# Where a finished sum is copied, when raw weights are loaded, and what stands in front of transpositions: three edits to a grouped-attention and Mish kernel

## The chip, the cores and the metric

The kernel runs on one core of a Trainium2 chip. A core has five engines that each take their instructions in the order of their own queue: TensorE (PE in the profile; PEld is its weight load), VectorE (DVE), ScalarE (ACT), GpSimd (POOL) and SyncE (SP), which here issues the DMAs. They tell each other by semaphores. Matrix products are written to PSUM, eight banks of 128 partitions x 512 floats; everything else lies in SBUF. The metric is the time of one execution in microseconds (us); a run's figure is compared with runs of the kernel before on the same chip.

## The reference, cut to what matters

```python
xn = layernorm(A_x)                              # 2048 x 512
q = xn @ wq; k = xn @ wk; v = xn @ wv            # 32 heads of 16; one k and v for all heads
p = softmax(q k^T / 4)                           # 32 x 2048 x 2048
s = (p v, heads side by side) @ wo               # 2048 x 512
h = xn @ w1 + b1                                 # 2048 x 1792
g = silu((h * tanh(softplus(h))) @ w2)           # Mish between the layers
out = A_x + s * g
```

All is float32. A dense product is kept precise by splitting both operands into a high and a low part and adding three partial products (`TERMS`), so a group of four 128-row weight blocks is 12 matrix products.

## The kernel before, in words

**Attention.** Queries are cut in 4 chunks of 512 rows (`C`) and 8 groups of 4 heads, so there are 32 passes ("heads" below, index v). A pass has 16 steps; in a step PE makes four score products `e` (line 966), four products `m` (L994) whose row maxima DVE takes (L998) for a pass that comes later, and the value products `pv` (L1050) of two steps before. ACT takes the exponential of each score (L971) into one of 14 tiles `pts`. The value products of a pass accumulate over its 16 steps in one PSUM bank. That pool, `ps_v`, has one buffer: the next pass's first value products can only start when the sum of the pass before has been read out. `o_out` does this: a copy on ACT (L1059, `os<-pv`), eight small DMAs out of `os` on SP (L1068), and, three steps later, jobs for ACT and POOL that divide by the row sums.

**Dense work.** The projections, both layers of the Mish branch and the output projection run as groups of 12 or 15 products (`xps`, L113 for a whole product, L117 for half of one). They are laid between the attention's products: a half of 64 rows runs beside a score or maximum product, which also uses 64 rows. A group of 12 takes four single steps, 6 halves in each; a group of 15 takes a "unit", four steps written out as two halves (`UNIT`). A group's `post` reads its sum out by ACT or DVE. Groups start at steps divisible by four and come from two queues, query groups first.

**The order.** The whole order is made by a Python planner when the program is built. Each engine has a list; steps, due times (`at`, `later`) and estimated times of POOL (`busy`) and SP (`sp_t`) say when something is emitted. The engines then run their lists in order.

**Weights.** Weights are loaded raw (`rawwq`, `rawws`, `rawwb`: two buffers together, `RAWS = 2`, at most one for each kind), split into a high part and a low part (in the lead-in by ACT and POOL, later by POOL alone, L165 and L170) and, in the main loop, stored split in DRAM, so that later chunks load them split. Split tiles sit in rings: 1 for `wq`, 2 for `ws` (first Mish layer), 5 for `wb` (second layer and output). Before the change `load` does nothing while the ring's next tile is still used by a group (`its[n - RING[tag]].users`), so the raw load of a first-layer block waits for the split tile of two blocks before. `pump` splits what has arrived and issues loads, once per step.

**The lead-in.** Up to about 91 us the planner works with `Task`s: statistics, scaling, transpositions of the input (`x_transpose`, 4 to a block, into the banks of `e`), key and value projection, value transpositions (`v_transpose`). PE takes, in this order of preference, a task, a pair of `m` products, or, where its next task is over 0.35 us away, three dense products ("X") or a warming product without use (`warm`, L1283). The main loop begins when 44 `m` products per side are through and the first pass's rows have been moved.

**Ends of passes.** In a single step, the last line of the step's branch calls `o_out` right after the pass's last value products. In a unit the first half does, after its last value products. The tail (the last 22 steps) has its own calls.

Of the kernel before, what the change touches and what calls it, by code (L numbers as in the profile page):

```python
# [36 lines left out]
X_US = 13.0  # L37
# [30 lines left out]
class Task:  # L68


    def __init__(self, eng, us, fn, deps=(), lat=0.1, at=0.0, prio=0):
        self.eng, self.us, self.fn, self.deps, self.lat, self.at, self.prio = eng, us, fn, list(deps), lat, at, prio
        self.end = None

# [49 lines left out]
def block_kernel(ctx: ExitStack, tc: tile.TileContext, x, wq, wk, wv, wo, w1, b1, w2, out):  # L124
# [13 lines left out]
    lead = {}  # L138
# [7 lines left out]
    def step_of(us):  # L146
        return base[0] + (us - base[1]) / STEP_US
# [248 lines left out]

    def arrived(tag):
        k, n = todo[tag]
        return k < n and items[tag][k].step + 1 <= (step[0] if lead else max(step[0], step_of(busy[0])) + 0.3)

    def home(tag, k):
# [22 lines left out]
    kept = {}  # L424
# [18 lines left out]
    def load(tag):  # L443
        its = items[tag]
        k, n = todo[tag]
        if tag == "wx" and m1_done.get((NC - 2, NFT - 1)) is None or lead and tag == "wq" and n > 1:
            return
        if n == len(its) or n >= RING[tag] and its[n - RING[tag]].users or lead and tag == "wb" and n and now[0] < kept_at.get(3, 1e9):
            return
        it = its[n]  # L450
        if n == k and kept.get(it.key):
            it.tile = home(tag, n)
            sp.dma_start(f(it.tile), kept[it.key])
            it.ready = math.ceil(2 * (sp_at(0.5) + 1.6)) / 2
            todo[tag][:] = n + 1, n + 1
        elif n - k < NRAW[tag] and raws[0] < RAWS:
            r = sb.tile([P, D], F32, tag="raw", name=f"raw{tag}{n}", bufs=RAWS)
            if len(it.src.shape) == 3:
                sp.dma_start(r.rearrange("p (t n) -> p t n", t=NDT), it.src)
            else:  # L460
                sp.dma_start(r, it.src)
            it.raw, it.step = r, (lead["arrive"]() if lead else sp_at(0.45))
            raws[0] += 1
            todo[tag][1] += 1

    def pump():
        for tag in items:
            while arrived(tag):
                split(tag)
            load(tag)  # L470

    held = [None]
    halves = [0]
# [127 lines left out]
    def unit(s, h):  # L601


        g, t = cur["g"], s + 2 * h
        xs = deque(g.mms)
        v, r = divmod(s, 16)
        es = deque((1 - h, r + j // 2, j % 2) for j in range(8))
        late = []
        relay = None

        def x_one():
            i = xs.popleft().half(cur["ps"], h)
            if len(xs) == len(g.mms) - 1 and h:
                tc.add_manual_dep(i.ins, cur["relay"].ins.name, mybir.DependencyInfo(
                    mybir.DependencyClass.Sync, mybir.DependencyReason.DATA), reason="other half of the bank")
            if h and g.dve and len(xs) == HOLD:
                held[0] = []
            if not xs and h:
                cur["n"] = len(g.mms)
                finish()  # L620
                for top in held[0] or ():
                    top()
                held[0] = None

        due(t)
        for n, op in enumerate(UNIT):
            if n == 8:
                due(t + 0.5)
                pump()
                due(t + 1)  # L630
            if op == "0":
                m_one(h)
                op = "E"
            elif xs:
                x_one()
            if op == "E":
                e = es.popleft()
                if len(es) > 1:
                    score(v, *e)()
                else:  # L640
                    late.append(score(v, *e))
            elif op in "Mm":
                relay = m_one(1 - h, op == "m")
        assert not xs and not es
        cur["relay"] = relay
        act_jobs(2 + (len(jobs) > 2))
        due(t + 1.5)
        for n in range(2):
            pv(t + n - 2)
            if n == 0:  # L650
                for fn in late:
                    fn()
        if t % 16 == 0:
            o_out((t - 16) // 16)

    qt_of = {}
    xt_done = {}
# [563 lines left out]
    for c0, c1 in ((0, 1), (1, 2), (2, 4)):  # L1221
        z = slice(4 * c0, 4 * c1)
        na = task("DVE", 0.2, lambda z=z: norm_a(z), st[z], prio=c0 and 1)
        nb = task("ACT", 0.45, lambda z=z: norm_b(z), [na])
        nrm = task("DVE", 0.8, lambda z=z: norm_c(z), [nb], prio=2 * c0 and 1)
        for c in range(c0, c1):
            xs, his = [], []
            for t in range(4 * c, 4 * c + 4):
                sc = task(*(("ACT", 0.72), ("DVE", 0.4))[c == 0], lambda t=t: x_scale(t), [nrm])
                tr = task("PE", 0.6, lambda t=t: x_transpose(t), [sc])  # L1230
                if c == 0:
                    hi = task("ACT", 0.55, lambda t=t: x_high(t), [tr])
                    lo = task("DVE", 0.65, lambda t=t: x_low(t), [hi])
                    bank("e", 3, tr, [lo])
                    xs.append(lo)
                else:
                    lo = task("ACT", 0.62, lambda t=t: x_copy(t), [tr])
                    bank("e", 3, tr, [lo])
                    xs.append(lo)
            los = xs  # L1240
            if c:
                his = [task("ACT", 0.98, lambda c=c, k=k: x_high2(c, k), xs, prio=2) for k in range(2)]
                los = [task("POOL", 2.5, lambda c=c, k=k: x_low2(c, k), [his[k]]) for k in range(2)]

            def xt_ok(c=c):
                xt_done[c] = step[0]
            if c < 2:
                task("POOL", 0.0, xt_ok, los)
            else:
                kept_0 = task("SP", 0.5, lambda c=c: xt_keep(c, 0), his)  # L1250

                def keep_low(c=c):
                    xt_keep(c, 1)
                    landed(2 * KEEP_US)
                    kept_at[c] = max(now[0] + 2, dma_t[0]) + 1
                task("SP", 0.5, keep_low, los + [kept_0])
            if c == 0:
                qp = task("PE", 2.8, lambda: fill(12), xs)
                xs = [qp]
            kus = 0.9 if c else 0.7  # L1260
            k0 = kp = task("PE", kus, lambda c=c: k_proj(c, (0,)), xs)
            for dt in range(1, 4):
                kp = task("PE", kus, lambda c=c, dt=dt: k_proj(c, (dt,)), [kp], lat=0.0)
            kv_done = kp
            kh = task("ACT", 0.59, lambda c=c: k_high(c), [kp])
            kl = task("DVE", 0.68, lambda c=c: k_low(c), [kh])

            def mv(c=c):
                k_move(c)
                kready[c] = now[0] + 2.6  # L1270
            moved = task("SP", 0.5, mv, [kl])
            if c == 0:
                lead["moved"] = moved
            vc = task("ACT", 0.59, lambda c=c: v_copy(c), [kp])
            bank("v", 1, k0, [kl, vc])
            vtr = task("PE", 0.5, lambda c=c: v_transpose(c), [vc])
            vo = task("DVE", 0.22, lambda c=c: v_out(c), [vtr])
            bank("v", 1, vtr, [vo])

# [25 lines left out]
    while True:  # L1305
# [58 lines left out]
        elif k == "J":  # L1364
            tag = next((g for g in ("wq", "ws", "wb") if arrived(g) and busy[0] + E0 < s + (4.5 if g == "ws" else 0.5)), None)
            n = ran[0]
            if tag:
                split(tag)
                T["ACT"] = s + 0.6
            else:  # L1370
                gap[0] = 0
                if not plan["POOL"]:
                    act_jobs(1)
                T["ACT"] = s + (0.65 if ran[0] > n else 0.15)
        else:
            plan[e].remove(k)
            k.fn()
            T[e] = max(s, T[e]) + k.us + (0.15 if e == "PE" and kind[0] == "M" else 0)
            k.end = T[e]
            if e == "PE":  # L1380
                kind[0] = "T"
# [30 lines left out]
    for s in range(NS + 2000):  # L1412
# [12 lines left out]
        if inm or cur["chunk"]:  # L1425
# [3 lines left out]

            def em(k):  # L1430
                n = m_sides(1 - h, k // 2) if inm else 0
                x = deque(lambda i=i: e_one(s, i) for i in range(4))
                y = deque(lambda: m_one(1 - h) for _ in range(n))
                r = [[], []]
                for op in EM:
# [12 lines left out]
            if s >= 2:  # L1448
                pv(s - 2)
                if (s - 1) % 16 == 0 and s > 1:  # L1450
                    o_out((s - 17) // 16)
        elif PAIRS[0] <= s < PAIRS[1]:
            due(s)
            if s % 2 == 0:
# [47 lines left out]
```

## Time and profile before

| | |
|---|---|
| median of 3 runs | 1587.54 us (1586.33 to 1588.32) |
| profiled execution | 1587.25 us, span 1585.5 us |
| granted TensorE clock | 0.996 of full speed |
| busy share of the span | PE 99%, PEld 55%, DVE 85%, ACT 82%, POOL 39% |
| chain that ended last | PE 93%, ACT 2%, DVE 2% |
| DMA | 126.76 MB, mean 80 GB/s |

In a row of the timeline stand: start in us from the span's start, length in us, engine, line, operation, tiles written and read, shapes, count, and in brackets the idle time before it and what ended that. A row of the windows has the window, its length, and for PE, PEld, DVE, ACT and POOL the busy us with the count of instructions, then the granted clock, the DMA share and GB/s. In the chain a row is start, length, engine, tile and line. A source row has the shortest, median and longest duration in ns, then the first and last start.

### The profile page before, as it was taken

Reading aid. Unit: us, or ns where it says so; the run is one execution under the profiler, and the core shown is the slowest. Engines: PE = TensorE matmul, PEld = TensorE weight load, DVE = VectorE, ACT = ScalarE, POOL = GpSimd, SP = SyncE. Lnnn points to the kernel's source line nnn. Section 1 sums busy time; section 2 is a strip of 40 time slices with the busy share of each in tenths; the row PEclk is TensorE's granted clock in tenths of the full one; section 3 lists DMA queues with packets and bytes.
Section 4 is the critical chain, followed back from the end, with each engine's and each line's share of the span. In section 5 each row is a group of like instructions: output and inputs, shape, how many; then the busy total and the mean of one; then the engine's idle time right before and its main releaser. Section 6 shows DMA issues by size and latency. Waiting matters only on the chain.

```text
span 1585.5 us, 31218 instructions
## 1 busy us (share of the span) xinstructions
PE 1567.0 (99%) x11649; PEld 876.2 (55%) x11649; DVE 1342.0 (85%) x2299; ACT 1296.2 (82%) x2492; POOL 622.6 (39%) x630
## 2 busy tenths in 40 slices
PE   8999999999999999999999999999999999999998
PEld 5455655665555565565555556556655555655643
DVE  8988887888988988888899988888889999888821
ACT  5469878878989787887988888798798888879786
POOL 3787527617446221450542323054044232405212
PEclk9999999999999999999999999999999999999999
DMA  5432114224132133311302231142221313121110
GB/s 163 147 105 85 58 47 131 84 58 144 41 122 70 55 104 97 112 41 49 109 23 97 85 100 34 49 161 95 71 84 32 105 53 107 29 71 58 32 63 27
DMA packets 73158, 126.76 MB, mean 80 GB/s; under 512 B 21488, under 2 KB 34800, under 8 KB 72496
## 3 DMA queue, kind: packets, MB, share of 16 engines
q1 hardware_dynamic: 73008, 124.78, 25.2%
q8 instruction: 92, 1.51, 0.4%
q14 instruction: 58, 0.48, 0.1%
HBM read 75.83 MB, written 27.26 MB: 65 GB/s over the span
## 4 chain that ended last, share of the span: by engine, by line
PE 93%; ACT 2%; DVE 2%; POOL 1%; DMA 1%; issue 0%; SPq 0%; DVEq 0%; POOLq 0%; ACTq 0%
PE xps L117 42%; PE pv L1050 31%; PE m L994 12%; PE e L966 6%; PE xps L113 2%; ACT pts L971 1%; DVE mb L998 1%; PE kp L309 1%; PE wop L113 1%; ACT pts L212 0%; PE warm L1283 0%; DMA pts<-in_dram 0%; DVE st L234 0%; DMA rawws<-in_dram 0%; PE xp L270 0%
## 5 line engine op out<-in xcount | busy, mean ns | idle before, releaser
L998 DVE TENSOR_REDUCE mb<-m 128x1 f32<-128x512 f32 x2048 | 1266.0, 681 | 171.5 <-PE m L994 112.1
L971 ACT ACTIVATE pts<-e 128x512 f32<-128x512 f32 x2042 | 1062.2, 606 | 217.7 <-PE e L966 152.4
L994 PE MATMUL m<-ks,qt 48*128 48x512 f32 (+1 forms) x2048 | 842.8, 427 | 0.6 <-DVE mb L998 0.3
L966 PE MATMUL e<-qt,ks 64*128 64x512 f32 x2048 | 746.4, 408 | 4.3 <-ACT pts L971 3.6
L1050 PE MATMUL pv<-pts,vaug 128*32 128x512 f32 x4084 | 530.8, 603 | 0.0
L994 PEld LDWEIGHTS m<-ks,qt 48*128 48x128 f32 (+1 forms) x2048 | 368.0, 185 | 115.6 <-DVE mb L998 67.3
L966 PEld LDWEIGHTS e<-qt,ks 64*128 64x128 f32 x2048 | 371.9, 186 | 28.9 <-ACT pts L971 16.9
L117 PE MATMUL xps<-xt,ws 64*128 64x512 f32 x1230 | 341.4, 410 | 0.2 <-POOL ws L170 0.2
L117 PEld LDWEIGHTS xps<-xt,ws 64*128 64x128 f32 x1230 | 212.0, 185 | 202.5 <-ACT pts L971 133.3
L117 PE MATMUL xps<-wbs,act 64*128 64x512 f32 x1248 | 313.5, 396 | 0.0
L117 PEld LDWEIGHTS xps<-wbs,act 64*128 64x128 f32 x1248 | 226.8, 185 | 63.5 <-ACT pts L971 29.3
L1050 PEld LDWEIGHTS pv<-pts,vaug 128*32 128x32 f32 x4084 | 88.1, 108 | 151.7 <-issue 143.7
L180 POOL TENSOR_SCALAR t<-t 128x512 f32<-128x512 f32 x56 | 34.4, 614 | 298.0 <-ACT t L732 298.0
L170 POOL TENSOR_TENSOR hb<-hb,t 128x512 f32<-128x512 f32 x56 | 72.2, 1289 | 120.5 <-ACT t L745 68.4
L117 PE MATMUL xps<-xt,wq 64*128 64x512 f32 x336 | 94.3, 414 | 0.0
L117 PEld LDWEIGHTS xps<-xt,wq 64*128 64x128 f32 x336 | 58.7, 187 | 55.5 <-ACT pts L971 36.9
L117 PE MATMUL xps<-wbs,ot_all 64*128 64x512 f32 x288 | 79.3, 408 | 0.0
L117 PEld LDWEIGHTS xps<-wbs,ot_all 64*128 64x128 f32 x288 | 49.5, 184 | 46.9 <-ACT pts L971 28.5
L170 POOL TENSOR_TENSOR act<-hb,act 128x512 fp32r<-128x512 f32 x56 | 72.2, 1289 | 4.7
L170 POOL TENSOR_TENSOR hb<-hb,u 128x512 f32<-128x512 f32 x56 | 72.3, 1290 | 4.4
L170 POOL TENSOR_TENSOR u<-u,t 128x512 f32<-128x512 f32 x56 | 71.8, 1283 | 4.7
L170 POOL TENSOR_TENSOR oc<-oc,sc 128x512 f32<-128x512 f32 (+1 forms) x16 | 20.6, 1288 | 103.0 <-ACT sc L1078 63.0
(122 smaller groups left out, 821.0 us busy)
## 6 DMA issues: line engine op xcount, KB each, us to landing
ws<-w SPq DMA_DIRECT2D x36, 512.0 KB
wbs<-w SPq DMA_DIRECT2D x35, 512.0 KB
qt<-qh SPq DMA_DIRECT2D x256, 32.0 KB
w<-wbs SPq DMA_DIRECT2D x14, 512.0 KB
wq<-wq SPq DMA_DIRECT2D x14, 512.0 KB
w<-ws SPq DMA_DIRECT2D x14, 512.0 KB
wbs<-wo SPq DMA_DIRECT2D x12, 512.0 KB
rawwb<-in_dram SPq DMA_DIRECT2D x21, 256.0 KB
```

The source lines that it names most:

```text
L113: self.pe.matmul(ps, self.lhs(), self.rhs(), start=(self.k == 0), stop=(self.k == self.tot - 1))
L117: i = self.pe.matmul(ps, self.lhs()[o], self.rhs()[o], start=(self.k == 0 and self.halves == 0), stop=(self.k == self.tot - 1 and self.hal ...
L170: eng.tensor_tensor(out=o, in0=a, in1=b, op=op)
L180: pool.tensor_scalar(o, o, lim, 0.0, op0=ALU.min, op1=ALU.max)
L309: pe.matmul(kp_of[c], wkf[:, dt], xf_of[c][dt // 2][:, dt % 2], start=(dt == 0), stop=(dt == 3))
L966: pe.matmul(e, ks[o:o + 64, P * k:P * (k + 1)], q[o:o + 64, p], start=True, stop=True)
L971: x = act.activation(dst, e, AF.Exp, scale=0.25)
L994: pe.matmul(m, q[o, p, P * t:P * (t + 1)], ks[o, C * kb:C * (kb + 1)], start=True, stop=True)
L998: return dve.reduce_max(out=mb_of[v][:, kb, z:z + 1], in_=m, axis=AX.X)
L1050: pe.matmul(o[32 * j:32 * j + 32], vaug[:, k], pt, start=(k == 0), stop=(k == 15))
```

## The change: what it does

It has three parts.

1. A `Task` gets a mark `fill`. It is set for the input transpositions of chunks 1 to 3 and the value transpositions of chunks 1 to 3. When the planner emits such a task on PE and a dense group is running, or one may begin, it emits one dense product in front of it and charges 0.25 us.
2. `load` goes on for first-layer weights (`ws`) that must be loaded raw, though the split tile is still used; `arrived` now says no while it is used, so the split alone waits.
3. `o_out` is no longer called where a pass ends, but put into a queue. In single steps the next step takes it from there before its third score; in units the next half takes it after all its scores, maxima and dense halves, ahead of ACT's jobs and the half's value products. The tail's own calls stay.

```diff
-    def __init__(self, eng, us, fn, deps=(), lat=0.1, at=0.0, prio=0):
+    def __init__(self, eng, us, fn, deps=(), lat=0.1, at=0.0, prio=0, fill=False):
+        self.fill = fill
...
     def arrived(tag):
         k, n = todo[tag]
+        if k >= RING[tag] and items[tag][k - RING[tag]].users:
+            return False
...
-        if n == len(its) or n >= RING[tag] and its[n - RING[tag]].users or lead and tag == "wb" and n and now[0] < kept_at.get(3, 1e9):
+        if n == len(its) or lead and tag == "wb" and n and now[0] < kept_at.get(3, 1e9):
             return
         it = its[n]
+        taken = n >= RING[tag] and its[n - RING[tag]].users
+        if taken and (tag != "ws" or kept.get(it.key)):
+            return
...
+    outs = deque()
+
+    def put_out(fn):
+        outs.append(fn)
+
+    def take_out():
+        if outs:
+            outs.popleft()()
...
         assert not xs and not es
         cur["relay"] = relay
+        take_out()
         act_jobs(2 + (len(jobs) > 2))
...
         if t % 16 == 0:
-            o_out((t - 16) // 16)
+            put_out(lambda: o_out((t - 16) // 16))
...
-                tr = task("PE", 0.6, lambda t=t: x_transpose(t), [sc])
+                tr = task("PE", 0.6, lambda t=t: x_transpose(t), [sc], fill=c > 0)
...
-            vtr = task("PE", 0.5, lambda c=c: v_transpose(c), [vc])
+            vtr = task("PE", 0.5, lambda c=c: v_transpose(c), [vc], fill=c > 0)
...
             plan[e].remove(k)
+            if k.fill and (cur["g"] is not None or not waiting and begun[0] < 1 + (s - 18) / X_US):
+                fresh = cur["g"] is None
+                if not fresh or begin():
+                    begun[0] += fresh
+                    fill(1)
+                    T[e] = max(T[e], s - 0.2) + 0.25
             k.fn()
...
-                x = deque(lambda i=i: e_one(s, i) for i in range(4))
+                x = deque(lambda i=i: (i == 2 and take_out(), e_one(s, i))[1] for i in range(4))
...
                 if (s - 1) % 16 == 0 and s > 1:
-                    o_out((s - 17) // 16)
+                    put_out(lambda s=s: o_out((s - 17) // 16))
```

## The prediction

> **What bounds the kernel now.** I read the page first (span, busy shares, chain), then the PE and ACT timelines around one handover of the value sum, then the stretches where a step is longer than its neighbours, then the lead-in by windows.
>
> ```profile
> span 1585.5 us, 31218 instructions
> PE 1567.0 (99%) x11649; PEld 876.2 (55%) x11649; DVE 1342.0 (85%) x2299; ACT 1296.2 (82%) x2492; POOL 622.6 (39%) x630
> PE 93%; ACT 2%; DVE 2%; POOL 1%; DMA 1%; issue 0%; SPq 0%; DVEq 0%; POOLq 0%; ACTq 0%
> ```
>
> PE is busy 99% of the span and 93% of the chain: outside the two ends there is no slack on PE, so any wait put on it is paid. The profiled execution took 1587.25 us (span 1585.5, 1.75 around it); the median of three is 1587.54. My sum runs against 1587.25.
>
> An ordinary step, and the handover of a head's finished sum, on PE (value products) and then on ACT:
>
> ```profile
> 425.12 1.07 PE L1050 MATMUL pv<-pts,vaug 128*32 128x512 f32 x8
> 426.46 0.39 PE L966 MATMUL e<-qt,ks 64*128 64x512 f32 x1
> 427.97 1.06 PE L1050 MATMUL pv<-pts,vaug 128*32 128x512 f32 x8
> ...
> 424.04 2.06 ACT L971 ACTIVATE pts<-e 128x512 f32<-128x512 f32 x4 [0.29 <-PE e L966]
> 426.26 0.60 ACT L1059 ACTIVATE os<-pv 128x512 f32<-128x512 f32 x1
> 426.90 2.06 ACT L971 ACTIVATE pts<-e 128x512 f32<-128x512 f32 x4
> ```
>
> A step lasts 2.85 us (425.12 to 427.97). The products at 425.12 finish a head; ACT copies them out at 426.26 to 426.86, in a hole: the first score of the next step is only there when the exponentials start at 426.90. The products at 427.97 belong to the next head and write the same, only PSUM buffer (pool `ps_v`, one buffer), so they must wait for that copy; today it is over 1.11 us before.
>
> **Part 3, the copy behind scores.** In single steps (L1471) `o_out` is queued and issued before the third score of the next step, so ACT runs exponential, exponential, copy, exponential, exponential. Four exponentials take 2.06 us; with 0.60 for the last one their starts lie (2.06 - 0.60)/3 = 0.487 apart. The third place begins at 426.90 + 2 x 0.487 = 427.87, the copy ends at 428.47, PE wanted 427.97: 0.50 us, and 0.05 for the signal (score ends on PE at 426.46 + 0.39 = 426.85, ACT starts at 426.90): 0.55 us. Queued behind it: on ACT two exponentials, whose tiles are read two steps later, so harmless; on PE everything, being in order, so the 0.55 us is paid. On SP the eight small DMAs out of `os` move 1.6 us later; they feed a job that is three steps off.
>
> ```profile
> L1059 ACT ACTIVATE os<-pv x31: 597/598/608, 143.3 to 1533.9; 128x512 f32<-128x512 f32 x31
> ...
> 187.92 1.85 PE pv L1050 x16
> 1487.33 1.85 PE pv L1050 x16
> ```
>
> There are 31 such copies. One, at 1533.9, is in the tail and stays. Eight fall in units (four steps in two halves, value products x16 in the chain; first and last head end shown, counted by the copies that follow). The other 22 are single: 22 x 0.55 = 12.1 us.
>
> In a unit `take_out` stands at the end of the next half, after six exponentials and, if the group's result goes through ACT, after that copy too:
>
> ```profile
> 181.90 1.92 PE L1050 MATMUL pv<-pts,vaug 128*32 128x512 f32 x16
> 187.85 1.92 PE L1050 MATMUL pv<-pts,vaug 128*32 128x512 f32 x16
> ...
> 189.90 0.61 ACT L1059 ACTIVATE os<-pv 128x512 f32<-128x512 f32 x1
> 190.38 3.07 ACT L971 ACTIVATE pts<-e 128x512 f32<-128x512 f32 x6
> 193.72 0.60 ACT L791 ACTIVATE y<-xps 128x512 f32<-128x512 f32 x1 [0.27 <-PE xps L117]
> ...
> 193.93 1.92 PE L1050 MATMUL pv<-pts,vaug 128*32 128x512 f32 x16
> ```
>
> A half takes 5.95 us (181.90 to 187.85), with the handover 6.08 (to 193.93): today's copy costs 0.13, which is saved. But `y` waits for the last dense product at 193.72, and `os` would run behind it, 194.3 to 194.9: the next value products start near 194.95 instead of 193.93, +1.0 us. Without `y` six exponentials and the copy end before PE asks: -0.13. The first third's groups (`y` by ACT) are four units in a row, and every fourth unit is a head's end, so one handover per chunk of 512 has it: 4 x 1.0 - 4 x 0.13 = +3.5 us. Part 3 together: +15.6 us. Bounds: 8 (the copy starts 0.2 us sooner everywhere, no `y` collision) to 18.
>
> Beside this row stands a rule of the Trainium skill, "TensorE: Matmul & The Clock Gate", part 1, on queue depths: ScalarE is strictly first in, first out, only TensorE may pull weight loads ahead. It speaks against this part, since the copy cannot overtake the two exponentials; the trace agrees (copy 426.26, then exponentials 426.90, in program order). If ACT could reorder, the part would cost nothing.
>
> **Part 2, raw first-layer weights ahead.** `load("ws")` no longer waits for a free split tile; only the split does (`arrived`). Where this matters shows in one place:
>
> ```profile
> 238.48 0.62 POOL L165 TENSOR_SCALAR ws<-rawws 128x512 fp32r<-128x512 f32 x1
> ...
> 252.26 0.40 SPq L459 DMA_DIRECT2D rawws<-in_dram  x1
> ...
> 256.06 0.62 POOL L165 TENSOR_SCALAR ws<-rawws 128x512 fp32r<-128x512 f32 x1 [6.82 <-DMA rawws<-in_dram]
> ...
> 262.67 0.72 ACT L741 ACTIVATE t<-u,two 128x512 f32<-128x512 f32 x1 [3.17 <-POOL u L170]
> ...
> 263.93 0.50 PE L966 MATMUL e<-qt,ks 64*128 64x512 f32 x1 [2.52 <-ACT pts L971]
> ...
> 258.52:264.36 5.84, 3.32 (x25) 1.59 (x23) 4.21 (x10) 2.67 (x7) 5.51 (x7) 1.00 0.85 314
> 264.36:268.64 4.28, 4.28 (x23) 2.32 (x23) 2.07 (x3) 3.01 (x7) 3.96 (x5) 0.62 0.00 1
> ```
>
> The load left SP only at 252.26; POOL stood 6.82 us before the split, ACT 3.17 us behind POOL's `u`, PE 2.52 us behind ACT, and the granted clock then fell to 0.62. Two steps took 5.84 + 4.28 = 10.12 instead of 5.70: 4.4 us. With the change this load is issued right after the split before it (POOL ran that at 238.48), on SP ahead of what it stood behind, and so lands some ten us earlier. I take the whole 4.4; bounds 0 (another transfer is late next: `wbs` or `wq`, now that `ws` sits on one of the two raw buffers) and -5. The cost on SP: a load may wait there for its raw buffer with `qt` pieces behind it; those are issued steps ahead, so 0, at most +2 if one is late.
>
> **Part 1, dense products before transpositions.** 12 input and 3 value transpositions each get one product in front where a group can run.
>
> ```profile
> 36.70:40.10 3.40, 2.60 (x17) 1.70 (x15) 3.30 (x6) 3.36 (x9) 0.00 (x0) 1.00 0.22 49
> 40.10:46.90 6.80, 6.80 (x19) 2.82 (x19) 4.39 (x9) 6.03 (x12) 3.99 (x3) 0.50 0.22 65
> 29.00:82.60 53.60, 50.93 (x194) 23.44 (x194) 49.73 (x86) 31.16 (x58) 36.38 (x28) 0.94 0.36 125
> 16.50 2.94 PE xps L113 x12
> 27.98 0.67 ACT L415 ACTIVATE ws<-rawws 128x512 fp32r<-128x512 f32 x1
> 84.07 2.87 PE L1283 MATMUL warm<-qt 128*128 128x512 f32 x9
> ```
>
> From 29 to 82.6 us the lead-in is paced by DVE's maxima (49.73 of 53.60 busy). Of its 3.9 us idle, 2.4 lie at 40.1 to 46.9 (6.80 - 4.39), where the clock is 0.50 after 3.4 us in which PE was busy 2.60 only. Two or three products there fill that hole; I take the clock as kept and the lead-in 2.4 us shorter. Bounds: -3.9 (all of DVE's idle time) and +3.6 (15 products at 2.94/12 = 0.24, every one in PE's way). In all about twelve products move forward, one group, some into the time of the nine warming ones at 84.07; the main loop takes a group each four steps, so the last group ends four steps earlier, in the tail:
>
> ```profile
> 1521.30:1531.90 10.60, 10.25 (x62) 4.45 (x60) 0.69 (x1) 9.88 (x21) 1.89 (x2) 1.00 0.09 26
> 1551.40:1562.50 11.10, 11.10 (x65) 4.51 (x64) 0.00 (x0) 9.86 (x20) 1.89 (x2) 1.00 0.01 1
> ```
>
> Four steps of the tail take 10.6 to 11.1 with ACT busy 9.9: without dense work ACT is next, so the gain is 0.7 to 1.2; I take 1.0, bounds 0 and -2.9 (all twelve).
>
> The skill's same page, part 4, says that transposes do not count as PE activity for the clock. Its rule would make products in front of them the right cure; the window 40.1 to 46.9 (0.50 while PE is busy 6.80 of 6.80) agrees in its direction.
>
> **Sum.** 1587.25 + 15.6 - 4.4 - 2.4 - 1.0 = 1595.05, 1595 us, 0.5% slower.
>
> **Rivals.** (a) The handover costs nothing, because the copy is done when PE asks: only a start of ACT's two exponentials 0.55 us sooner would do it. 1587.25 - 0.5 - 4.4 - 2.4 - 1.0 = 1579. Against it stands the even 0.487 us spacing, paced by PE's scores. It decides at (7.8 - 3.5)/22 = 0.2 us a handover: below that, the change gains. (b) The stall at 258 us stays or moves to another late transfer: 1595 + 4.4 = 1599.5. For it: two raw buffers for three users; against: SP had the time. (c) The products find no ready group, or the clock falls all the same: 1595 + 2.4 + 1.0 = 1598.5. For it: the second group's weights are split only at 27.98, and PE is nearly full from 30 to 60 us already. (d) Gains at their far ends, 3.9 and 2.9, and no `y` collision: 1595 - 1.5 - 1.9 - 4.0 = 1587.6, no change.
>
> **How the numbers follow.** Forecast 0.50 (1591 to 1598), (a) 0.12, (b) 0.15, (c) 0.15, (d) 0.08. Slower by more than 0.2% (3.2 us, about what a measurement tells from none): 0.50 + 0.15 + 0.15, less 0.04 for the forecast's low edge: 0.76. Same: 0.08 + 0.04 = 0.12; faster 0.12. Leaving out (a) and the ends of the bounds, 1587 to 1603.
>
> **What would show it.** Right: after a single handover the `os` copy sits between the second and third exponential and the next head's value products start 3.4 us after the last ones, with `os` named as their releaser, 22 times; four unit halves of 7 us; no 6.82 us of POOL idle; clock 1.00 at 40 us; one more `ws` group before the main loop. Wrong: handover steps of 2.85 us (rival a), or a new stall elsewhere in the first 300 us.

## The result, and the profile after

The changed kernel takes 1611.41 us (median of 5 runs, 1610.38 to 1616.03), the kernel before in the same series 1586.33: a ratio of 1.0159, with an interval of 1.0143 to 1.0176. It is slower, as forecast, but by 25 us and not by 8, and outside the range of 1587 to 1603. The profiled execution took 1612.26 us, its span is 1610.5.

From the page of the changed kernel: the span, the busy shares, the chain by engine, and from the groups by line that of the value products (busy time and mean; behind the bar the idle time ahead of it and what ended that). The last row is the same group in the kernel before.

```profile
span 1610.5 us, 31225 instructions
PE 1573.3 (98%) x11643; PEld 874.9 (54%) x11643; DVE 1345.8 (84%) x2299; ACT 1295.1 (80%) x2492; POOL 623.3 (39%) x630
PE 92%; ACT 4%; DVE 1%; issue 1%; POOL 1%; DMA 1%; ACTq 0%; SPq 0%; DVEq 0%; POOLq 0%
L1066 PE MATMUL pv<-pts,vaug 128*32 128x512 f32 x4084 | 533.1, 605 | 14.7 <-ACT os L1075 14.7
...
L1050 PE MATMUL pv<-pts,vaug 128*32 128x512 f32 x4084 | 530.8, 603 | 0.0
```

In the chain PE's share went from 93% to 92% and ACT's from 2% to 4%, and the value products, which waited for nothing before, now wait 14.7 us for the copy `os`. That is one of three places where the time went. I split both traces at the starts of the value products: of step 0 (the end of the lead-in), of step 486 (the start of the tail) and the last one. Steps are counted here by sets of value products, and the third set is step 0 (104.7 us in the kernel before); the first two sets, from 98.83 us on, belong to the lead-in. "Step 53" is the interval from the start of its set to the next.

| stretch, us | before | after | difference | forecast |
|---|---|---|---|---|
| lead-in, up to step 0 | 104.7 | 114.1 | +9.4 | -2.4 (part 1) |
| steps 0 to 486 | 1409.9 | 1427.0 | +17.1 | +11.2 (parts 2 and 3) |
| tail, from step 486 | 57.4 | 56.0 | -1.4 | -1.0 |
| end, behind the last value product | 13.4 | 13.4 | 0 | 0 |

**The handover (part 3).** Timeline of the changed kernel, PE and then ACT, one single handover:

```profile
434.03 1.06 PE L1066 MATMUL pv<-pts,vaug 128*32 128x512 f32 x8
437.42 1.06 PE L1066 MATMUL pv<-pts,vaug 128*32 128x512 f32 x8 [0.48 <-ACT os L1075]
...
435.79 1.09 ACT L987 ACTIVATE pts<-e 128x512 f32<-128x512 f32 x2 [0.78 <-PE e L982]
436.77 0.60 ACT L1075 ACTIVATE os<-pv 128x512 f32<-128x512 f32 x1
437.24 1.11 ACT L987 ACTIVATE pts<-e 128x512 f32<-128x512 f32 x2
```

Two exponentials, the copy, two exponentials: the copy ends at 437.37, the next head's products start at 437.42, and the step is 3.39 us long instead of 2.85, as forecast.

**The old stall (part 2).** The stretch that held it, in the changed kernel: first POOL's split from the timeline, then a window (length, busy us and count of PE, PEld, DVE, ACT and POOL, granted clock, DMA share, GB/s).

```profile
252.72 0.61 POOL L166 TENSOR_SCALAR ws<-rawws 128x512 fp32r<-128x512 f32 x1
...
258.50:268.60 10.10, 10.10 (x84) 5.37 (x80) 8.99 (x16) 9.35 (x19) 9.60 (x11) 1.00 0.55 168
```

POOL's 6.82 us of idle time and the half clock are gone. The window is the one at the same time, and the changed kernel runs later; the steps that were long before, 53 and 54, now start at 270.92 and 273.76 and take 2.85 us each. But 300 us later a unit, step 155, is late in a way that the kernel before does not show at all:

```profile
571.60 0.49 PE L118 MATMUL xps<-wbs,act 64*128 64x512 f32 x1 [0.86 <-DMA wbs<-w]
...
574.09 0.50 PE L118 MATMUL xps<-wbs,act 64*128 64x512 f32 x1 [1.53 <-DMA wbs<-w]
...
574.99 3.60 PE L1066 MATMUL pv<-pts,vaug 128*32 128x512 f32 x16
```

PE waits twice for second-layer weights that come back from DRAM, and its sixteen value products then take 3.60 us instead of 1.92, at half clock.

**The lead-in (part 1).** The same window, first of the kernel before, then of the changed one:

```profile
26.00:106.00 80.00, 75.46 (x317) 36.76 (x319) 73.50 (x131) 48.66 (x94) 56.98 (x48) 0.96 0.34 112
```

```profile
26.00:106.00 80.00, 72.40 (x273) 35.84 (x273) 70.62 (x120) 42.55 (x81) 50.47 (x41) 0.91 0.30 97
```

DVE, which paces this part, gets through 120 instructions instead of 131, and TensorE's granted clock is 0.91 instead of 0.96. Where it begins is seen on DVE, POOL, ACT and PE of the changed kernel, with the window behind it:

```profile
30.00 2.47 DVE L1014 TENSOR_REDUCE mb<-m 128x1 f32<-128x512 f32 x4
32.40 2.17 DVE L242 SCALAR_TENSOR_TENSOR hv<-ve,rstd 128x8 f32<-128x8 f32 x1
34.60 2.27 DVE L171 TENSOR_TENSOR hv<-hv,rstd 128x8 f32<-128x8 f32 x1
...
32.17 4.68 POOL L171 TENSOR_TENSOR xt<-xf,xt 128x1024 fp32r<-128x1024 f32 x2 [0.87 <-ACT xt L295]
...
37.31 2.93 ACT L213 ACTIVATE pts<-pts,nbias,rstd 128x512 f32<-128x512 f32 x4 [4.27 <-DVE nbias L242]
...
37.93 0.50 PE L1010 MATMUL m<-ks,qt 64*128 64x512 f32 x1 [2.97 <-DVE mb L1014]
...
39.10:52.80 13.70, 13.70 (x43) 7.82 (x42) 8.93 (x15) 9.62 (x19) 2.75 (x3) 0.50 0.07 19
```

The kernel before, DVE and POOL at the same place:

```profile
29.96 1.27 DVE L998 TENSOR_REDUCE mb<-m 128x1 f32<-128x512 f32 x2
31.16 0.15 DVE L241 SCALAR_TENSOR_TENSOR hv<-ve,rstd 128x8 f32<-128x8 f32 x1
31.34 0.17 DVE L170 TENSOR_TENSOR hv<-hv,rstd 128x8 f32<-128x8 f32 x1
...
32.12 2.39 POOL L170 TENSOR_TENSOR xt<-xf,xt 128x1024 fp32r<-128x1024 f32 x1 [2.11 <-ACT xt L294]
```

Two steps of the normalisation, 128x8 elements each, took 0.15 and 0.17 us before. Now they take 2.17 and 2.27 us, each as long as one of POOL's two subtractions of 128x1024 (4.68 / 2 = 2.34) that run beside it. The new order lets two further maxima run ahead of them on DVE, so they come 1.24 us later, at 32.40 instead of 31.16, and POOL has begun at 32.17. The scaling of the next chunk on ACT waits for them (4.27 us), PE stands 2.97 us for the maxima that are queued on DVE behind them, and from 39.1 us on the clock is 0.50 for 13.7 us.

### The profile page after: what moved, and what is told of

It is laid out like the page before. It is cut to its first block, busy times and chain, and to the rows that moved or that the text cites. A ratio compares the mean times of both kernels' runs of the same rounds, so it can differ in the third digit from the quotient of the medians.

```text
span 1610.5 us, 31225 instructions
## 1 busy us (share of the span) xinstructions
PE 1573.3 (98%) x11643; PEld 874.9 (54%) x11643; DVE 1345.8 (84%) x2299; ACT 1295.1 (80%) x2492; POOL 623.3 (39%) x630
## 4 chain that ended last, share of the span: by engine, by line
PE 92%; ACT 4%; DVE 1%; issue 1%; POOL 1%; DMA 1%; ACTq 0%; SPq 0%; DVEq 0%; POOLq 0%
PE xps L118 41%; PE pv L1066 31%; PE m L1010 11%; PE e L982 6%; PE xps L114 2%; ACT pts L987 2%; ACT os L1075 1%; DMA wbs<-w 0%; PE wop L114 0%; PE xp L271 0%; POOL wbs L171 0%; PE kp L310 0%; DMA pts<-in_dram 0%; DVE st L235 0%; ACT hb L742 0%
## 5 line engine op out<-in xcount | busy, mean ns | idle before, releaser
L1066 PE MATMUL pv<-pts,vaug 128*32 128x512 f32 x4084 | 533.1, 605 | 14.7 <-ACT os L1075 14.7
L118 PE MATMUL xps<-xt,ws 64*128 64x512 f32 x1212 | 336.3, 410 | 0.0
```

The costliest lines, as they stand in the source:

```text
L118: i = self.pe.matmul(ps, self.lhs()[o], self.rhs()[o], start=(self.k == 0 and self.halves == 0), stop=(self.k == self.tot - 1 and self.hal ...
L1066: pe.matmul(o[32 * j:32 * j + 32], vaug[:, k], pt, start=(k == 0), stop=(k == 15))
```

## The experiments

Diffs are against the changed kernel unless said otherwise. In the table the main part of each profiled execution is cut at the value products of steps 0, 22, 86, 150, 182 and 486. The old stall lies in 22 to 86, the new one in 150 to 182.

| kernel | median us | ratio to before, interval | lead-in | 0-22 | 22-86 | 86-150 | 150-182 | 182-486 | tail |
|---|---|---|---|---|---|---|---|---|---|
| before | | | 104.7 | 63.3 | 191.4 | 182.9 | 93.4 | 878.9 | 57.4 |
| whole change | 1611.41 | 1.0159 [1.0143, 1.0176] | 114.1 | 65.0 | 188.7 | 185.1 | 99.4 | 888.8 | 56.0 |
| part 1 alone | 1597.65 | 1.0064 [1.0052, 1.0077] | 109.6 | 63.4 | 191.8 | 182.9 | 93.4 | 879.0 | 57.5 |
| part 2 alone | 1588.62 | 1.0016 [1.0007, 1.0025] | 104.9 | 64.4 | 186.7 | 182.9 | 98.5 | 880.3 | 56.0 |
| part 3 alone | 1597.29 | 1.0068 [1.0056, 1.0080] | 103.1 | 63.9 | 189.4 | 185.1 | 94.9 | 888.5 | 57.5 |
| parts 1 and 2 | 1596.72 | 1.0062 [1.0049, 1.0075] | 121.4 | 64.4 | 186.7 | 182.9 | 99.2 | 880.1 | 56.0 |
| part 1, norm first | 1586.13 | 1.0001 [0.9992, 1.0010] | 103.1 | 63.4 | 192.2 | 182.8 | 93.4 | 878.9 | 57.5 |
| part 1, POOL in quarters | 1587.91 | 1.0010 [1.0002, 1.0019] | 104.8 | 63.4 | 191.4 | 183.0 | 93.4 | 878.9 | 57.5 |
| part 2, later | 1581.72 | 0.9974 [0.9963, 0.9985] | 105.9 | 63.3 | 187.3 | 183.1 | 93.4 | 878.7 | 57.4 |
| part 2, patient | 1583.42 | 0.9983 [0.9975, 0.9992] | 107.4 | 64.4 | 186.7 | 182.9 | 92.8 | 878.9 | 57.4 |
| part 3, singles, second score | 1585.10 | 0.9997 [0.9988, 1.0005] | 104.7 | 63.5 | 188.0 | 183.5 | 93.4 | 880.3 | 57.4 |
| part 3, units only | 1589.20 | 1.0023 [1.0012, 1.0034] | 104.6 | 63.3 | 192.0 | 182.9 | 94.4 | 880.6 | 57.4 |
| part 2 later, part 1 norm first | 1581.56 | 0.9970 [0.9958, 0.9982] | 103.0 | 63.4 | 187.2 | 183.0 | 93.4 | 879.0 | 57.5 |
| whole change, norm first | 1601.48 | 1.0095 [1.0081, 1.0108] | 104.1 | 65.0 | 189.1 | 185.1 | 99.2 | 888.8 | 56.0 |

The lead-in column is to be read with care: it holds what half-clock stretches that execution happened to have, which differ between executions of one kernel (parts 1 and 2 together ran from 1594.15 to 1605.84 us, at mean granted clocks of 0.995 to 0.987, and the profiled execution was the 1605.84). Each kernel has one trace, so how much the other columns move between executions of one kernel is not shown; between kernels they agree closely where the copies stand alike (86 to 150: 182.8 to 183.1 in the ten kernels that copy in single steps as before).

### Part 3 alone

The two lines that set `fill=c > 0` and the three edits in `arrived` and `load` are taken back.

> Part 3 alone: the copies of the finished sums are taken late, the lead-in and the loads are those of before. Theory A (every part costs what its own wait costs): 22 single handovers at +0.55 us, 4 unit handovers behind a y copy at +1.0, 4 others at -0.1, so +15.6 us, 1602 us. Rival B (the whole loss is the copy, because late sums also disturb what follows): +25 us, 1611 us. Rival C (the lead-in is the whole loss): 1587 us.

Median 1597.29, +11.2 us. Groups by line, and a window of its lead-in:

```profile
L1061 PE MATMUL pv<-pts,vaug 128*32 128x512 f32 x4084 | 531.6, 604 | 14.7 <-ACT os L1070 14.7
...
40.10:46.90 6.80, 6.80 (x25) 2.70 (x24) 6.41 (x12) 5.88 (x12) 4.89 (x3) 1.00 0.35 124
```

PE waits the same 14.7 us for the copy as in the whole change, 22 times in single steps of 3.40 us and four times in units of about 7.0 us, so the price of part 3 is its own. Its main part is only 11.9 us longer than before, because the old stall shrank by some 4 us (the step at s=53 is 3.30 us): the eight DMAs out of `os`, which the copy moves back, now stand on SP behind a raw load of second-layer weights instead of ahead of it (that load is issued at 243.77, before at 249.20), and POOL is through with it before the late one comes.

The second row bears on the clock. Up to here the lead-in has the instructions of the kernel before, and yet the clock stays at 1.00 where the kernel before, in its profiled execution, had 0.50. The drop that the forecast meant to fill is not in every execution.

### Part 1 alone

`put_out` calls its function at once, and `load` and `arrived` are as before:

```diff
     def put_out(fn):
-        outs.append(fn)
+        fn()
```

> Part 1 alone: dense products in front of transpositions, copies and loads as before. Theory A: this part makes the lead-in longer (in the changed kernel the first value product starts at 107.3 instead of 98.8 us, with DVE's small operations held for 4.4 us beside POOL's two 128x1024 subtractions and the clock at half after that): +8.5 us, less 1 in the tail, 1594 us, and the first value product near 107 us. Rival: the longer lead-in comes from the raw loads taking the two buffers (part 2): this kernel is at 1584 us with the first value product at 96 us.

Median 1597.65, +11.5 us. 1594 was expected, with the first value products near 107 us; in the traced execution they start at 102.82. The two normalisation steps take 2.18 and 2.34 us here too, from 32.38 and 34.60, and PE stands 3.05 us for the maxima behind them. The main part and the tail are as before (1410.6 against 1409.9, and 57.5): the whole loss lies in the lead-in, which in this, its fastest, execution (1592.83) was 4.9 us longer. The other four took 1597.13 to 1598.32 us at a mean granted clock of 0.988 to 0.990, this one had 0.994; they left no trace, so where their further 4 to 5 us lie is not shown. The dense products ahead of step 0 come to 87 full ones, as before: part 1 moves them within the lead-in and brings none of the main loop's forward.

### Part 2 alone, and parts 1 and 2

Part 2 alone: `put_out` at once, and no `fill`. Parts 1 and 2: `put_out` at once.

> Part 2 alone: raw first-layer weights loaded ahead, copies and products as before. Theory A: POOL's 6.8 us wait for a raw load near 250 us and the two long steps after it go, -4.4 us: 1582 us, lead-in as before (first value product at 98.8 us). Rival: with one raw buffer always held, second-layer weights come late (the changed kernel has a step of 7.84 instead of 5.09 us at 567 us, PE waiting for a DMA into wbs): 1587 us or more. Rival 2: the longer lead-in is this part's: 1591 us.

> Parts 1 and 2 together, copies where they were. Theory A: the changed kernel less the handovers' 16.5 us (22 x 0.55, 5 x 1.0, some units 0.1 better), 1595 us; first value product near 107 us. Rival B (all the loss is the copy): 1583 us or less.

Part 2 alone is 2.5 us slower than before. In its table row the old stall is worth -4.7 (22 to 86), and it is eaten by +5.1 at 150 to 182, +1.1 in the first 22 steps and +1.4 after step 182. The tail is 1.4 shorter; ahead of step 0 there are 99 dense products instead of 87 (two halves counted as one), one group. Timeline of PE, and of SP's queue, of part 2 alone:

```profile
557.88 0.49 PE L118 MATMUL xps<-wbs,act 64*128 64x512 f32 x1 [1.14 <-DMA wbs<-w]
...
560.83 0.50 PE L118 MATMUL xps<-wbs,act 64*128 64x512 f32 x1 [1.97 <-DMA wbs<-w]
...
551.92 0.68 SPq L459 DMA_DIRECT2D wbs<-w  x1
...
553.16 0.38 SPq L459 DMA_DIRECT2D wbs<-w  x1
```

One group more ahead of the main loop means that each dense group comes one slot earlier, so this unit begins at s=155 and not at s=159. It begins before its weights are there. Three loads go out, at 551.48, 551.92 and 553.16; by the profile PE's two waits end when the second and the third have landed, so these are used 557.88 - 551.92 = 6.0 us and 560.83 - 553.16 = 7.7 us after they went out, while the planner (`it.ready` in `load`) counts on 1.6 steps, 1.6 x 2.85 = 4.6 us. A store and another load of 512 KB each went out among them and right behind, and from 552 to 561 us the DMA engines were 89% busy. The loads read split weights back and need no raw buffer, so a raw buffer that is taken does not explain the delay. Parts 1 and 2 together show the same late unit, 9.13 us. Their main part is 3.3 us longer than before, so of the whole change's +17.1 part 3 has 1427.0 - 1413.2 = 13.8.

### Part 1 with the normalisation first

In the lead-in's planner a pair of maxima is held back until DVE's last normalisation step has been emitted (parts 2 and 3 taken back):

```diff
+        if len(m_ends) > 5 and nrm.end is None:
+            return None
```

> Part 1 alone (1597.65 us) with one order undone: the second and further m pairs wait in the plan until VectorE's last normalising operations are emitted, so these run before POOL's two 128x1024 subtractions, as in the kernel before. Theory A (VectorE's operations with two SBUF operands were held by POOL's whole instruction, 2.2 + 2.3 us, and the clock fell behind that): both operations take 0.2 us, the first value product comes 4 us or more sooner than 102.8 us, total 1590 us, within 3. Rival (the dense products themselves stretch the lead-in, 15 x 0.24 = 3.6 us on PE): the operations are short, but the time stays at 1595 to 1598 us.

DVE and POOL, and the window of the lead-in:

```profile
31.16 0.15 DVE L242 SCALAR_TENSOR_TENSOR hv<-ve,rstd 128x8 f32<-128x8 f32 x1
31.34 0.17 DVE L171 TENSOR_TENSOR hv<-hv,rstd 128x8 f32<-128x8 f32 x1
...
32.13 2.39 POOL L171 TENSOR_TENSOR xt<-xf,xt 128x1024 fp32r<-128x1024 f32 x1 [0.88 <-ACT xt L295]
...
29.00:82.60 53.60, 52.69 (x205) 24.37 (x203) 52.60 (x91) 31.15 (x58) 38.86 (x30) 1.00 0.37 124
```

The same window of part 3 alone, whose lead-in has none of part 1's products:

```profile
29.00:82.60 53.60, 50.92 (x203) 24.36 (x202) 52.01 (x91) 31.61 (x59) 38.73 (x30) 1.00 0.37 129
```

Median 1586.13: all of part 1's 11.5 us are gone, by an order that moves these steps 1.2 us forward. The planner's other choices move with it: of POOL's two subtractions the second now comes at 44.13 us, about where the kernel before has it (43.33). In the window DVE is busy 52.60 us where it was 49.73, at a clock of 1.00, and the first value products start at 96.05, 2.8 us sooner than before. But that is not shown to be part 1's doing: in part 3 alone, where the clock happened to stay at 1.00 in this window as well, DVE is busy 52.01 us with as many instructions and the first value products start at 96.39. Nor does the lead last: from 93.3 the clock is 0.50 for 6.8 us, and step 0 stands at 103.1, as in part 3 alone. In the median nothing of it is left.

### Part 1 with POOL's subtraction in quarters

The order stays that of part 1; only each of POOL's subtractions of 128x1024 is cut into four (parts 2 and 3 taken back):

```diff
-        sub(pool, xt_of[c][:, 1, 2 * k:2 * k + 2], xf_of[c][k], f(xt_of[c][:, 0, 2 * k:2 * k + 2]))
+        charge(1.3)
+        for j in range(2):
+            for z in (slice(0, C // 2), slice(C // 2, C)):
+                pool.tensor_tensor(out=xt_of[c][:, 1, 2 * k + j, z], in0=xf_of[c][k][:, j, z],
+                                   in1=f(xt_of[c][:, 0, 2 * k + j, z]), op=ALU.subtract)
```

> Part 1 alone with POOL's subtractions for the input chunks written as four of 256 elements each, the order unchanged. Theory A (VectorE waits for the POOL instruction that is running): the two held operations take about 0.6 us each instead of 2.2 and 2.3, ACT's 4.4 us wait for nbias shrinks to about 1.5, total 1594 us. Rival (VectorE waits for something else of that length, a DMA or a semaphore): they keep 2.2 and 2.3 us, 1597 us.

DVE and POOL of this kernel, and the wait on PE, first of part 1 alone, then of this kernel:

```profile
32.30 0.54 DVE L242 SCALAR_TENSOR_TENSOR hv<-ve,rstd 128x8 f32<-128x8 f32 x1
32.87 0.66 DVE L171 TENSOR_TENSOR hv<-hv,rstd 128x8 f32<-128x8 f32 x1
33.56 0.65 DVE L242 SCALAR_TENSOR_TENSOR rstd<-hv,rstd 128x8 f32<-128x8 f32 x1
34.24 0.65 DVE L242 SCALAR_TENSOR_TENSOR nbias<-mvs,rstd 128x8 f32<-128x8 f32 x1
...
32.07 5.57 POOL L301 TENSOR_TENSOR xt<-xf,xt 128x256 fp32r<-128x256 f32 x8 [0.88 <-ACT xt L295]
...
38.00 0.79 PE L1005 MATMUL m<-ks,qt 64*128 64x512 f32 x1 [3.05 <-DVE mb L1009]
...
35.54 0.49 PE L1009 MATMUL m<-ks,qt 64*128 64x512 f32 x1 [0.70 <-DVE mb L1013]
```

The DVE steps still come late and are still held, but now all four, and each for 0.54 to 0.66 us, the length of one quarter (5.57 / 8 = 0.70). So a step is held for one whole instruction of POOL's, at both lengths that were tried; that is shown. PE's stop shrank from 3.05 to 0.70 us, and the time came back further than the 3.7 us expected, 9.7 of 11.5 us: with the shorter stop the clock stayed at 1.00 up to 94.8 us. That points to the clock, more than to the stop itself, as what makes part 1 dear; it is argued from these figures and not shown by a run of its own.

The Trainium skill has this rule, "SBUF — State Buffer", section "Who interferes with whom": a VectorE instruction with two SBUF inputs and a GpSimd instruction that reads SBUF exclude each other, and the one issued first keeps the other out for its whole length, while the reductions of VectorE are never kept out. The traces agree on both: in the whole change 2.17 and 2.27 us against 0.15 and 0.17 before, and four maxima in 2.47 us beside POOL's splits.

### Part 2, later and patient

Later: raw loads ahead only from the 13th first-layer block on. Patient: part 2 everywhere, but a block that uses second-layer weights is planned one step further behind their load. Both without parts 1 and 3.

```diff
-        if taken and (tag != "ws" or kept.get(it.key)):
+        if taken and (tag != "ws" or kept.get(it.key) or n < 12):
```

```diff
-            it.ready = math.ceil(2 * (sp_at(0.5) + 1.6)) / 2
+            it.ready = math.ceil(2 * (sp_at(0.5) + (2.6 if tag == "wb" else 1.6))) / 2
```

> Part 2 alone, but loads go ahead only from the thirteenth first-layer block on, so that nothing moves before 230 us. Theory A: part 2 does what it is for, and its loss (1588.62) came from groups moving up by four steps into late second-layer weights: the two long steps near 258 us go (-4.4 us), no step of 8.8 us near 553 us, 1582 us. Rival (a held raw buffer starves the others wherever it is used): a new late transfer, 1586 us or more.

> Part 2 alone, and the planner is told that the split and transposed first-layer weight is ready one step later than it thinks now, so that it puts the block that uses it one step further behind the load. A, the unit near s=155 waits because the transfer of wbs is late by about one step there: that unit falls from about 8.8 back to about 5.1 us, and the whole is some 3.7 us below the 1588.6 us of part 2 alone: 1585 us. B, the transfers move along with the load (the queue itself is late): a step of over 7 us stays somewhere near it, 1588 us or above.

Both are faster than the kernel before, by 0.26% and 0.17%. Begun later, part 2 leaves the early groups in their old slots, and its row in the table is that of the kernel before but for the old stall: 187.3 instead of 191.4. So the mechanism that the forecast gave to part 2 is there and worth 4 us. The patient kernel, SP's queue and the first product of that unit on PE:

```profile
553.94 1.55 SPq L459 DMA_DIRECT2D wbs<-w  x2
...
556.07 0.38 SPq L459 DMA_DIRECT2D wbs<-w  x1
...
567.83 0.40 PE L118 MATMUL xps<-wbs,act 64*128 64x512 f32 x1
```

The loads are issued at the same steps as in part 2 alone, but the unit starts 567.83 - 553.94 = 13.9 us behind the first of them. The recorded text speaks of first-layer weights there, but the edit delays second-layer ones (`wb`). I had expected the unit one step later; the planner found no other block for s=155 to 158 and put it at s=159, its slot in the kernel before. The four steps without dense products in between take 2.71 to 2.75 us each, and the tail is back at 57.4, so the group gained ahead of the main loop is given back here. What is shown is that starting the unit too soon behind its loads made the new stall.

### Part 3 at other places

In singles ahead of the second score, with units as before; and in units only, with singles as before (parts 1 and 2 taken back in both):

```diff
-                x = deque(lambda i=i: (i == 2 and take_out(), e_one(s, i))[1] for i in range(4))
+                x = deque(lambda i=i: (i == 1 and take_out(), e_one(s, i))[1] for i in range(4))
```

```diff
-                    put_out(lambda s=s: o_out((s - 17) // 16))
+                    o_out((s - 17) // 16)
```

> Part 3 in single steps alone, the copy before the second score instead of the third; units as before. Theory A (the next pass's value products wait for the copy, and its place in ScalarE's queue sets how long): the copy ends 0.49 us sooner than in the third place, handovers cost 0.05 to 0.1 us instead of 0.55, 22 of them 1 to 2 us; with the 4 us that the late copy alone gained near 258 us, 1584 us (1583 to 1588). Rival (any late copy costs its 0.6 us): 1586 + 22 x 0.55 - 4 = 1594 us.

> Part 3 in the units only; at the single steps the copy stands where it stood before. A, the price of the copy behind the third score lies in both kinds of step, and in the units falls on the halves with a load of y: four unit handovers at about 7.01 us where they were 6.08, the others at about 6.01, the single handovers at 2.85 as before, the sum +3.5 us: 1589 to 1590 us. B, the longer unit steps of the whole change come from something else (another transfer, the clock), and the copy costs nothing there: 1586 us or below, no unit step near 7.01.

Behind one exponential, PE and ACT:

```profile
422.10 1.07 PE L1061 MATMUL pv<-pts,vaug 128*32 128x512 f32 x8
425.01 1.06 PE L1061 MATMUL pv<-pts,vaug 128*32 128x512 f32 x8
...
424.37 0.59 ACT L1070 ACTIVATE os<-pv 128x512 f32<-128x512 f32 x1
```

Units only, ACT and PE, and its group of value products:

```profile
193.67 0.60 ACT L802 ACTIVATE y<-xps 128x512 f32<-128x512 f32 x1 [0.41 <-PE xps L118]
194.17 0.59 ACT L1070 ACTIVATE os<-pv 128x512 f32<-128x512 f32 x1
...
194.81 0.64 PE L1061 MATMUL pv<-pts,vaug 128*32 128x512 f32 x4 [1.00 <-ACT os L1070]
...
L1061 PE MATMUL pv<-pts,vaug 128*32 128x512 f32 x4084 | 531.5, 604 | 4.0 <-ACT os L1070 4.0
```

One place earlier in the queue, the copy ends at 424.96 and the products start at 425.01: a step of 2.91 instead of 3.40 us. The price falls by 0.49 us, the time of the one exponential that no longer stands ahead of it. Here, too, the DMAs move on SP and shorten the old stall (188.0 against 191.4), which pays for what is left of the price. In units the collision with `y` is as forecast: copy at 194.17, 1.00 us of waiting, a step of 7.01 to 7.03 us, four times; the main part is 3.3 us longer, where 3.5 were expected.

### Two sums

Part 2 later together with part 1 with the normalisation first; and the whole change with the normalisation first.

> Part 1 with the last normalisation steps of the lead-in ahead of further pairs of maxima, and part 2 from the 13th first-layer block on, the copies of finished sums as before the change. A, the two repaired parts add: 1581.7 us of part 2 begun late and no more from part 1 (its lead of 2.8 us is paid back by a half-clock stretch later): 1580 to 1583 us, the step at s=53 at about 2.9 us and no step of 8 us. B, a shift of the lead-in brings a new late transfer: 1585 us or above, with a step of 7 us or more that neither part alone has.

> The whole change, with the last normalisation steps of the lead-in ahead of further pairs of maxima on VectorE. A, the lead-in's 9.4 us come from those steps being held beside GpSimd's long subtraction and from the half clock behind it: both go, 8 to 11 us less than the whole change: 1600 to 1603 us. B, in the whole change the lead-in is late for another reason (the loads of part 2, the clock alone): 1608 us or above.

Both came out as theory A had it. The first is at 1581.56, 0.30% faster than before, and can't be told from part 2 later by itself; the repaired part 1 adds nothing. The second, DVE and the window of its lead-in:

```profile
31.09 0.15 DVE L242 SCALAR_TENSOR_TENSOR hv<-ve,rstd 128x8 f32<-128x8 f32 x1
...
26.00:106.00 80.00, 75.04 (x329) 36.47 (x331) 73.68 (x132) 50.27 (x96) 59.07 (x50) 1.00 0.32 103
```

1601.48: two lines of order give back 9.9 of the 25 us, all in the lead-in (104.1 instead of 114.1, at a clock of 1.00 where the whole change had 0.91). The rest is the main part, 1427.3, with its handovers and its late unit.

## Why the prediction was wrong

Its own terms against what the traces of before, of the whole change and of parts 1 and 2 give:

| term | forecast | measured | where it is read |
|---|---|---|---|
| part 3, handovers | +15.6 | +13.8 | main part, whole change less parts 1 and 2; 14.7 of waiting in the group row |
| part 2, old stall | -4.4 | -4.7 | part 2 alone, steps 22 to 86 |
| part 2, what is late next | 0 | +8.0 | parts 1 and 2: main part +3.3, less the -4.7 |
| part 1, lead-in | -2.4 | +9.4 | lead-in |
| tail | -1.0 | -1.4 | tail |

1587.25 + 13.8 - 4.7 + 8.0 + 9.4 - 1.4 = 1612.35, against 1612.26 measured. The rows are differences of the same few traces, so the sum closes by construction; it shows where the time lies, and the experiments show why.

- **Part 3 was right**, in its mechanism and nearly in its size: 0.55 us a single handover, 0.93 to 0.95 us (7.01 to 7.03 against 6.08) where `y` is in the way. The whole change has 20 such single steps and not 22, and five unit handovers behind `y` and not four. Counted by handovers that is 20 x 0.55 + 5 x 0.94, less 5 x 0.07 for the other units (6.01 against 6.08), 15.4 us; the difference of 13.8 is smaller because the first step of the late unit took 7.84 us here and 9.13 in parts 1 and 2. What the forecast called harmless, eight DMAs on SP a little later, was a gain when part 3 was alone: it took some 4 us off the old stall. Rival (a), a free handover, is refuted.
- **Part 2's step "I take the whole 4.4" failed** for want of its other side. The stall went. But the same edit brought one more group ahead of step 0, moved every group up by a slot, and a unit met its second-layer weights 3 us too soon. The forecast had named `wbs` as the next late transfer, though for want of a raw buffer, and rival (b) priced it at 4.4; it cost 8.0 with the smaller losses (7.5 in part 2 alone). The two runs that put the groups back into their old slots, from the start (1581.72) or from that unit on (1583.42), show that this is what ate the gain.
- **Part 1's step "I take the clock as kept and the lead-in 2.4 us shorter" failed.** It looked at PE, ACT and DVE's idle time and priced the products on PE (at most +3.6). It didn't ask in which order DVE's own instructions would then come, nor what ran on POOL beside them. What the runs showed in its place: two normalisation steps came behind POOL's subtractions and were held 2.17 and 2.27 us, PE stood 2.97 us, the clock was then 0.50 for 13.7 us, and the lead-in was 9.4 us longer. Nor did the gain itself show when the order was repaired: the first value products came 2.8 us sooner than before, but only 0.3 us sooner than in part 3 alone, which has no such products and whose clock stayed at 1.00 up to 95.6 us, and the median didn't gain. Against rival (c), which let the products do nothing, the lead-in lost 9.4.
- **The tail was right in size by luck and wrong in cause.** The forecast put it down to part 1's products. Part 1 alone leaves the tail at 57.5 and brings no dense product more ahead of step 0; part 2 alone has 99 instead of 87 there, and the tail of 56.0.
- **On the clock** the forecast took the 0.50 at 40.1 us, seen in one execution, for a property of the kernel. Part 3 alone has 1.00 there with the same lead-in. So the rule cited from the Trainium skill, "TensorE: Matmul & The Clock Gate", part 4, on transpositions, gets no verdict: the clock was kept there without products in front of transpositions (part 3 alone) and lost with them (the whole change).

What stays open: which idle time on PE costs a half-clock stretch. Away from the end of the span they come in lengths of 3.4 us and its multiples (3.4, 6.8, 13.7, 17.1), and kernels with the same instructions up to there have them at different places: the kernel before from 40.1 us, part 3 alone only from 95.6. No run here separates what decides it. The same page of the Trainium skill, part 1, "What's actually happening", says that the gate looks at a free-running window of about 3.4 us, so that where a kernel's work falls in it differs from run to run. The lengths seen here and the changing places agree with that; how much idle time within a window is too much, no run here shows.

## What to carry to other kernels

A product that is put in front of another instruction also changes the order on the engines that take its results; before pricing it, list what each of them will do next, and what a neighbour engine has in hand at that moment. A load that comes early moves more than the wait that it removes: everything that is planned by its arrival moves up, so look for the first block that then stands too close to its own loads. And a copy that frees the only buffer of a producer belongs as far ahead in its engine's queue as it can be: here the place behind two exponentials instead of one cost 0.49 us at every single handover, and behind one instead of none 0.06 (2.91 against 2.85), because the copy had been early.

## What the runs showed of the hardware that was not expected

- A VectorE instruction of 128x8 elements with two inputs in SBUF, 0.15 us by itself, takes 2.17 us when a GpSimd subtraction of 128x1024 (2.34 us) has begun before it, and 0.54 to 0.66 us when that subtraction is cut into pieces of 0.70 us.
- Part 1 alone stopped PE for 3.05 us and lost 11.5 us in the median; shortening the stop to 0.70 us gave 9.7 of them back, with a clock of 1.00 up to 94.8 us where part 1 alone had 0.50 from 37.9 us for 6.8 us.
- The same lead-in ran in one execution with the clock at 0.50 from 40.1 to 46.9 us (the kernel before) and in another at 1.00 up to 95.6 us (part 3 alone); its first value products started at 98.83 and 96.39 us.
- Three read-backs of 512 KB each went out within 2.1 us (551.48 to 553.54); beside a store and another load of that size, PE still waited for the second until 6.0 us and for the third until 7.7 us after its issue.
